# Eight key chunks per batch on VectorE and GpSimd, w2 in three loads, result columns in two PSUM tiles

## The chip, the core and the metric

The kernel runs on one core of a Trainium2 chip. The core has five engines that run side by side and meet at semaphores: TensorE (PE in the profile; its weight loads are listed as PEld), VectorE (DVE), ScalarE (ACT), GpSimd (POOL) and SyncE (SP), which here only issues transfers. Transfers between memory and SBUF are made by 16 DMA engines. A transfer of 128 rows is cut into 16 shares, one for each of them; this text calls the sixteen tracks on which these shares run one after the other *lanes*. TensorE writes to PSUM, and VectorE and ScalarE copy from there.

The metric is the device time of one execution in microseconds. Before the change three runs gave a median of 193.28 us (193.25 to 193.34).

## The reference

One decoding step for eight batch rows: a gated mix of an attention block and a small MLP, which read the same input.

```python
x = A_x                                     # [8, 1, 448]
g = sigmoid((x * gate_w).sum(-1))           # one gate per batch row
q = (x @ wq) as 16 heads of 256
k, v = the last 1024 positions of the caches, 8 heads, each used by 2 query heads
a = softmax(q k^T / 16) v, joined, @ wo
b = gelu(layernorm(x) @ w1 + b1) @ w2 + b2  # 448 -> 1792 -> 448
return g * a + (1 - g) * b                  # [8, 1, 448], bfloat16
```

The keys and values are 8 batches x 8 heads x 1024 positions x 256 numbers in bfloat16, 4 MB each per batch; wq, wo, w1 and w2 add 10.6 MB. In all 77.67 MB are read.

## The kernel before, in words

**Transfers.** All large loads go through SP's queue into a ring of four SBUF slots of 4 MB, in the order that the list `plan` gives: keys of batch 0, wq, then keys of batch b and values of batch b-1 by turns, then w1, the values of the last batch with w2 behind them, and wo. `pump` issues the next load when `done` has given a slot back. A key or value slot is filled by two loads of 2 MB (`kv_loader`, line 128), one for each group of four heads. w1, and later w2, share one slot (`w12`): w2 is issued by `last_values` (line 157) after the last values as one load of 128 rows of 12,544 B, into columns of that slot that nothing else uses. wo comes in seven pieces (line 140), the last four of them small, so that the last matmuls wait for little. Each load signals a semaphore; eight semaphores go round, and a load is issued only when the one eight places before it has landed.

**Keys.** `transpose_keys(b)` turns the keys of a batch so that the head dimension lies on the partitions. A batch has two halves of 32 chunks of 128 columns (`kn`, read as 4-byte words), and the work goes in 16 groups of four chunks (`CB = 4`). Groups 1 to 15 go through TensorE: four transposes into a PSUM tile `ktp` (line 360), then one copy to the SBUF tile `kt`, by ScalarE for the groups in `BY_ACT` (line 366) and by VectorE for the others (line 368). Group 0 goes another way, `turn_blocks`: VectorE turns 32x32 blocks into the tile `B` (line 330), and GpSimd puts the blocks in their places in `kt` with 16 copies (line 338). The steps of the softmax of the batch before are emitted between the groups, by the table `steps`: exp on ScalarE after group 0, its turning on VectorE after group 2, and so on.

**Attention.** `scores(b)` (line 427) multiplies the turned keys with the queries into `S_ps`; it needs all of `kt`. `top` takes the maximum on VectorE (`nmx`, line 440), `expo` the exponentials on ScalarE (`E`, line 444), `turn` turns them on VectorE (`EB`, line 451), `scale` and `bring` make the weights `ET`, and `values` (line 498) multiplies them with the values into `PO`. `finish` and `spread` (lines 511 to 524) put the result of a batch into `oP`.

**The tail.** After the last scores, `mlp_hidden` makes the hidden layer `hs`; `A1` is cleared (line 617); `values`, `finish` and `spread` end the last batch. Then the output matmuls run: 14 on w2 and 26 on wo, 448 columns wide, into `A1` on four row groups (line 632), whose sums VectorE takes to `accs` (line 639); then the last six chunks of wo, four matmuls of 112 columns each, and between them `accs` summed by `pick`, all into `A2` (line 643). `A2` holds the four column quarters on four groups of partitions. VectorE copies the first two quarters to `res0` and SP sends them; ScalarE copies the other two to `res1` and sends them from its own queue (lines 656 and 657).

Of the kernel before, what the change touches and what calls it, by code (L numbers as in the profile page):

```python
# [12 lines left out]
F32 = mybir.dt.float32  # L13
# [4 lines left out]
def kernel(  # L18
# [15 lines left out]
    nc = tc.nc  # L34
    P = nc.NUM_PARTITIONS

    NB, Sq, D = A_x.shape
# [8 lines left out]
    QD = 4  # L46
    BL = P // QD
# [7 lines left out]
    FB = FQ // BL  # L55
# [4 lines left out]
    SK = P // QD  # L60
    NCK = W // SK
    CB = 4
    UR = NG * rep
    HALF = D // 2
    DO = D // QD
# [16 lines left out]
    epool = ctx.enter_context(tc.tile_pool(name="epool", bufs=1))  # L82
# [3 lines left out]
    ps_kt = ctx.enter_context(tc.tile_pool(name="ps_kt", bufs=3, space=PSUM))  # L86
# [15 lines left out]
    def done(n=1):  # L102
        consumed[0] += n
        pump()
# [5 lines left out]
    def slot(*key):  # L110
        return slots[index[key]]

    def kv_loader(src, b, cuts=(1, 1), inner=False):
        pieces = [
            (i, k, cuts[i])
            for i in range(NG)
            for k in range(cuts[i])
        ]
        if inner:
            pieces.sort(key=lambda x: x[1])  # L120

        def load(t):
            for i, k, m in pieces:
                v = src[b, i * QD : (i + 1) * QD, kv_base:Sk, :].rearrange(
                    "a (s c) d -> s a (c d)", c=NCK
                )
                n = HS // m
                nc.sync.dma_start(  # L128
                    t[:, i * HS + k * n : i * HS + (k + 1) * n],
                    v[:, :, k * n : (k + 1) * n],  # L130
                )

        return load
# [15 lines left out]
    w2_v = B_w2.rearrange("(p c) n -> p (c n)", c=FB)  # L149
    wo_v = A_wo.rearrange("(q p j) n -> p q (j n)", p=P, j=J8)  # L150
    OW1T = NR * F
    OW2 = OW1T + FH
    wq_r = [wq_m[:, r * HD : (r + 1) * HD] for r in range(NR)]

    def last_values(t):
        kv_loader(A_v_cache, NB - 1, (2, 2), True)(t)
        nc.sync.dma_start(slot("w12")[:, OW2 : OW2 + FB * D], w2_v)

    add(("k", 0), kv_loader(A_k_cache, 0, (2, 1)))
    add(("wq",), rows_loader(wq_r + [wq_t]))  # L160
    for b in range(1, NB):
        add(("k", b), kv_loader(A_k_cache, b))
        add(("v", b - 1), kv_loader(A_v_cache, b - 1))
    add(("w12",), rows_loader([w1_m, w1_t]))
    add(("v", NB - 1), last_values)
    cuts = [(q, 0, J8) for q in range(NQW - 2)] + [
        (NQW - 2, 0, 4),
# [32 lines left out]
    nc.gpsimd.memset(xw[:], 0.0)  # L200
    qw = consts.tile([P, NJ, NB, QD, 2 * UR], BF16)
    nc.vector.memset(qw[:], 0.0)
# [120 lines left out]

    KT = {}

    BY_ACT = (1, 3, 4, 6, 7, 8, 10, 11, 13, 15)

    def turn_blocks(kn, kt, c0):
        B = epool.tile([P, CB, QD, SK // QD, QD], F32, tag="B", name="B")
        nc.vector.transpose(  # L330
            B[:].rearrange("p c w s a -> p (c w s a)"),
            kn[:, c0 * P : (c0 + CB) * P],
        )
        S8 = SK // QD
        words = kt[:].bitcast(F32)
        for w in range(QD):
            for g in range(QD):
                nc.gpsimd.tensor_copy(  # L338
                    words[BL * w : BL * (w + 1), :, c0 : c0 + CB, g * S8 : (g + 1) * S8, 0],
                    B[BL * g : BL * (g + 1), :, w].rearrange("p c s a -> p a c s"),  # L340
                )

    def transpose_keys(b, between=None):
        between = between or {}
        kn = slot("k", b)[:].bitcast(F32)
        for hh in range(NG):
            kt = ktpool.tile([P, QD, NCK, SK, NJ], BF16, tag="kt", name="kt")
            KT[hh] = kt
            for i in range(NCK // CB):
                g = hh * (NCK // CB) + i  # L350
                if g == 0:
                    turn_blocks(kn, kt, 0)
                    for step in between.get(g, ()):
                        step()
                    continue
                ktp = ps_kt.tile([P, CB, P, NJ], BF16, tag="ktp", name="ktp")
                words = ktp[:].bitcast(F32)
                for c in range(CB):
                    o = (hh * NCK + i * CB + c) * P
                    nc.tensor.transpose(  # L360
                        words[:, c, :, 0], kn[:, o : o + P], ident_f[:]
                    )
                dst = kt[:, :, i * CB : (i + 1) * CB, :, :]
                src = ktp[:].rearrange("p c (s a) t -> p a c s t", a=QD)
                if g in BY_ACT:
                    nc.scalar.copy(dst, src)  # L366
                else:
                    nc.vector.tensor_copy(dst, src)  # L368
                for step in between.get(g, ()):
                    step()  # L370
        done()
# [49 lines left out]
    def scores(b):  # L421
        CQ = QN // SK
        for n in range(W // QN):
            for u in range(NG):
                for j in range(NJ):
                    for t in range(QD):
                        nc.tensor.matmul(  # L427
                            S_ps[BL * t : BL * t + UR, n * QN : (n + 1) * QN],
                            lhsT=qw[:, j, b, t, rep * u : rep * u + UR],
                            rhs=KT[u][:, t, n * CQ : (n + 1) * CQ, :, j],  # L430
# [23 lines left out]
    def scale(b):  # L454
        EB = soft.pop(b)
        rs = spool.tile([P, BL], F32, tag="rs", name="rs")
        nc.vector.stream_shuffle(rs[:], EB[:, NCK, :], [0] * BL)
        sc = spool.tile([P, UR], F32, tag="sc", name="sc")
        nc.vector.reciprocal(sc[:], rs[:, 0:UR])
        nc.vector.tensor_scalar_mul(sc[:], sc[:], gall[:, b : b + 1])  # L460
        EZ = spool.tile([P, NCK, UR], BF16, tag="EZ", name="EZ")
        nc.vector.tensor_tensor(  # L462
# [117 lines left out]
    def steps(b):  # L580
# [15 lines left out]
        return d  # L596

    transpose_keys(0, {7: [moments]})
    gate()
    query()  # L600
    scores(0)
    top(0)
    for b in range(1, NB):
        transpose_keys(b, steps(b - 1))
        scores(b)
        top(b)
        values(b - 1)
# [11 lines left out]
    finish(b)  # L619
    spread(b)  # L620

    A2 = ps_kt.tile([P, DO], F32, tag="ktp", name="A2")
    w2 = slot("w12")
    w = slot("wo")
    NCH = NQW * J8
# [4 lines left out]
    for i, (lhsT, rhs) in enumerate(wide):  # L630
        g = i % QD
# [9 lines left out]
    for i, (lhsT, rhs) in enumerate(narrow):  # L641
        for t in range(QD):
            nc.tensor.matmul(
                A2[BL * t : BL * t + NB, :],
                lhsT=lhsT,
                rhs=rhs[:, t * DO : (t + 1) * DO],
                start=(i == 0),
                stop=(i == TAIL),
            )
    for h, (eng, copy) in enumerate(  # L650
        ((nc.sync, nc.vector.tensor_copy), (nc.scalar, nc.scalar.copy))
    ):
        res = consts.tile([NB, 2, DO], BF16, name=f"res{h}")
        for i in range(2):
            t = 2 * h + i
            copy(res[:, i, :], A2[BL * t : BL * t + NB, :])  # L656
        eng.dma_start(
            out_f[:, h * HALF : (h + 1) * HALF], res[:].rearrange("b i d -> b (i d)")
        )
# [30 lines left out]
```

## Time and profile before

| | before |
|---|---|
| median of three runs | 193.28 us |
| profiled execution's own time | 193.19 us |
| its span in the profile | 191.4 us |
| DMA: mean rate over the span | 407 GB/s |
| TensorE busy | 119.1 us (62%) |
| VectorE busy | 108.7 us (57%) |
| ScalarE busy | 91.9 us (48%) |
| GpSimd busy | 55.4 us (29%) |
| ScalarE's copies of turned keys, 80 of them | 76.1 us, mean 1024 ns |
| GpSimd's copies of turned keys, 128 of them | 51.3 us, mean 401 ns |
| VectorE's turn of group 0, 8 of them | 5.7 us, mean 711 ns |
| last piece of wo landed | 187.03 us |
| first and second half of the result landed | 189.47 and 190.06 us |

The times in the lower rows and in all profile lines are microseconds from the start of the span; the mean of one instruction is in nanoseconds. The page shows the span in 40 slices of 4.8 us: one digit for a slice is the busy share in tenths. q1 is SP's DMA queue, q10 ScalarE's; q8 and q14 are the queues that fetch instructions. A line of the timeline gives start, length, engine, line of the kernel, operation, output and inputs, count, and in brackets how long the engine had been idle before and what ended that. A line of the chain gives start, length and what the end of the kernel waited for then.

### The profile page before, as it was taken

The numbers are of one execution on the slowest core, as the hardware profiler recorded it, in microseconds if no ns is written. First come the engines' busy times: TensorE is split into PE (matmuls) and PEld (weight loads), VectorE is DVE, ScalarE is ACT, GpSimd is POOL, SyncE is SP. The second block draws the span as 40 slices with busy tenths as digits, with TensorE's granted clock in tenths as the row PEclk, the third lists the DMA queues.
The fourth block names the chain that finished last, engine by engine and source line by source line (L and its number), as shares of the span: only waits on it lengthen the run. The fifth ranks groups of instructions, "written<-read, shape, count | busy, mean of one in ns | idle before, by whom it ended". The sixth has DMA issues, their size and how long they took to land.

```text
span 191.4 us, 2916 instructions
## 1 busy us (share of the span) xinstructions
PE 119.1 (62%) x1114; PEld 77.0 (40%) x1114; DVE 108.7 (57%) x248; ACT 91.9 (48%) x105; POOL 55.4 (29%) x143
## 2 busy tenths in 40 slices
PE   0658509679784397738773676669854885083552
PEld 0646104555671185317641563168514761010111
DVE  4284673964889467705870687037822885847311
ACT  2298420894992259525852594228822892000001
POOL 8480000570750066005700480049002910000000
PEclk9999855999999969996999999756997999855555
DMA  5999999999999999999999999999999999999980
GB/s 204 445 402 425 440 435 419 425 421 432 422 430 428 428 421 431 426 431 428 418 431 425 421 435 428 428 428 416 431 431 428 425 425 420 403 422 430 407 321 3
DMA packets 7129, 77.86 MB, mean 407 GB/s; under 512 B 830, under 2 KB 1228, under 8 KB 1996
## 3 DMA queue, kind: packets, MB, share of 16 engines
q1 hardware_dynamic: 7072, 77.67, 96.3%
q8 instruction: 8, 0.13, 0.3%
q14 instruction: 5, 0.04, 0.1%
q10 hardware_dynamic: 44, 0.02, 0.0%
HBM read 77.67 MB, written 0.01 MB: 406 GB/s over the span
## 4 chain that ended last, share of the span: by engine, by line
DMA 73%; PE 10%; DVE 7%; ACT 4%; SPq 2%; issue 2%; DVEq 0%; ACTq 0%
DMA slot<-in_A_k_cache_dram 42%; DMA slot<-in_A_v_cache_dram 14%; DMA slot<-in_A_wq_dram 9%; DMA slot<-in_A_wo_dram 8%; PE ktp L360 7%; ACT kt L366 3%; DVE kt L368 2%; PE S_ps L427 2%; DVE qw L419 1%; SPq L128 1%; SPq L140 1%; DVE EZ L462 1%; PE S_ps L391 1%; DVE qt L404 1%; DVE nmx L440 1%
## 5 line engine op out<-in xcount | busy, mean ns | idle before, releaser
L366 ACT COPY kt<-ktp 128x1024 bf16<-128x1024 bf16 x80 | 76.1, 1024 | 37.0 <-PE ktp L360 36.9
L360 PE MATMUL ktp<-ident_f,slot 128*128 128x128 f32 x480 | 71.7, 305 | 31.4 <-DMA slot<-in_A_k_cache_dram 22.9
L360 PEld LDWEIGHTS ktp<-ident_f,slot 128*128 128x128 f32 x480 | 60.2, 157 | 49.2 <-issue 23.6
L338 POOL COPY kt<-B 32x128 f32<-32x128 f32 x128 | 51.3, 401 | 97.8 <-DVE B L330 86.3
L368 DVE COPY kt<-ktp 128x1024 bf16<-128x1024 bf16 x40 | 27.5, 689 | 16.9 <-PE ktp L360 16.5
L498 PE MATMUL PO<-slot,ET 128*16 128x512 bf16 x256 | 18.1, 429 | 16.2 <-DMA slot<-in_A_v_cache_dram 16.2
L444 ACT ACTIVATE E<-S_ps,nmx 128x1024 f32<-128x1024 f32 x8 | 8.9, 1114 | 28.7 <-DVE nmx L440 28.7
L330 DVE STREAM_TRANSPOSE B<-slot 128x512 f32<-128x512 f32 x8 | 5.7, 711 | 29.7 <-DMA slot<-in_A_k_cache_dram 29.6
L427 PE MATMUL S_ps<-kt,qw 128*4 128x512 bf16 x256 | 17.9, 419 | 5.4 <-DVE qw L419 5.4
L498 PEld LDWEIGHTS <-ET 128*16 128x16 bf16 x256 | 6.1, 94 | 27.6 <-DMA slot<-in_A_v_cache_dram 21.0
L440 DVE TENSOR_REDUCE nmx<-S_ps 128x1 f32<-128x1024 f32 x8 | 9.8, 1222 | 10.0 <-PE S_ps L427 10.0
L427 PEld LDWEIGHTS <-qw 128*4 128x4 bf16 x256 | 6.6, 85 | 14.0 <-DVE qw L419 6.5
L451 DVE STREAM_TRANSPOSE EB<-E 128x1056 f32<-128x1056 f32 x8 | 10.2, 1271 | 1.3 <-ACT E L444 1.3
L524 DVE TENSOR_TENSOR oP<-Y 32x32 bf16<-32x32 f32 x32 | 9.4, 295 | 1.1
L656 ACT CAST res<-A 8x112 bf16<-8x112 f32 x2 | 0.5, 246 | 15.8 <-DVE res L656 15.8
L481 DVE TENSOR_TENSOR ET<-sm,mask 128x512 bf16<-128x512 f32 x8 | 5.5, 692 | 2.2 <-PE sm L473 2.1
L511 DVE STREAM_TRANSPOSE T<-PO 128x512 f32<-128x512 f32 x8 | 5.7, 709 | 1.0 <-PE PO L498 0.9
L566 ACT ACTIVATE zb<-za 128x448 f32<-128x448 f32 x1 | 0.6, 577 | 10.8 <-DVE za L565 10.8
L473 PE MATMUL sm<-EZ,perm 128*128 128x128 bf16 x8 | 1.7, 216 | 6.0 <-DVE EZ L462 5.9
L632 PE MATMUL A<-slot,oP 128*8 128x448 bf16 x26 | 3.5, 547 | 2.5 <-DMA slot<-in_A_wo_dram 2.5
L639 DVE TENSOR_TENSOR accs<-A,b2s 128x448 f32<-128x448 f32 x1 | 0.6, 624 | 7.1 <-PE A L632 7.1
L516 DVE TENSOR_TENSOR Y<-T 64x64 f32<-64x64 f32 x16 | 4.0, 248 | 0.5
(91 smaller groups left out, 58.1 us busy)
## 6 DMA issues: line engine op xcount, KB each, us to landing
slot<-in_A_k_cache_dram SPq DMA_DIRECT2D x15, 2048.0 KB, 28.1
slot<-in_A_v_cache_dram SPq DMA_DIRECT2D x14, 2048.0 KB, 30.2
slot<-in_A_v_cache_dram SPq DMA_DIRECT2D x4, 1024.0 KB, 23.9
slot<-in_A_wq_dram SPq DMA_DIRECT2D x3, 1024.0 KB, 17.1
slot<-in_A_k_cache_dram SPq DMA_DIRECT2D x2, 1024.0 KB, 6.4
slot<-in_A_wo_dram SPq DMA_DIRECT2D x2, 896.0 KB, 18.7
slot<-in_B_w_dram SPq DMA_DIRECT2D x1, 1568.0 KB
slot<-in_B_w_dram SPq DMA_DIRECT2D x1, 1344.0 KB, 26.4
```

What stands on the lines that cost most here:

```text
L330: nc.vector.transpose(B[:].rearrange("p c w s a -> p (c w s a)"), kn[:, c0 * P : (c0 + CB) * P],)
L338: nc.gpsimd.tensor_copy(words[BL * w : BL * (w + 1), :, c0 : c0 + CB, g * S8 : (g + 1) * S8, 0], B[BL * g : BL * (g + 1), :, w].rearrange( ...
L360: nc.tensor.transpose(words[:, c, :, 0], kn[:, o : o + P], ident_f[:])
L366: nc.scalar.copy(dst, src)
L368: nc.vector.tensor_copy(dst, src)
L427: nc.tensor.matmul(S_ps[BL * t : BL * t + UR, n * QN : (n + 1) * QN], lhsT=qw[:, j, b, t, rep * u : rep * u + UR], rhs=KT[u][:, t, n * CQ ...
L440: nc.vector.reduce_max(nmx[:], S_ps[:], axis=AXIS.X, negate=True)
L444: nc.scalar.activation(E[:, 0:W], S_ps[:], ACT.Exp, bias=soft.pop(b)[:], scale=1.0, accum_out=E[:, W : W + 1],)
L451: nc.vector.transpose(EB[:].rearrange("p c r -> p (c r)"), E[:])
L498: nc.tensor.matmul(PO[BL * t : BL * t + Hq], lhsT=ET[:, c].rearrange("p u a r -> p (u a r)"), rhs=vn[:, c], start=(c < QD), stop=(c >= NCK ...
L511: nc.vector.transpose(T[:], PO[:].rearrange("p u (e j) -> p u j e", j=J8))
L524: nc.vector.tensor_tensor(oP[BL * i : BL * (i + 1), :, :, b], Yv[0:BL, :, :, i], Yv[BL : 2 * BL, :, :, i], op=ALU.add,)
```

## The change

Three edits.

1. VectorE and GpSimd take the first eight chunks of a batch's keys, two groups instead of one. `turn_blocks` works on `CP = 8` chunks: one turn of 1024 words per partition instead of 512, and 16 copies of 256 words instead of 128. Group 1 leaves `BY_ACT`, so TensorE transposes 14 groups and ScalarE copies nine; VectorE still copies five. The table `steps` has nothing for group 1.
2. w2 is loaded in three transfers: partitions 0 to 111, 112 to 119 and 120 to 127. Bytes and places are the same.
3. `A2` becomes two PSUM tiles. Quarters 0 and 1 go to the first, quarters 2 and 3 to the second, on the same partitions as before; VectorE copies from the first, ScalarE from the second.

```diff
+    CP = 8
...
     def last_values(t):
         kv_loader(A_v_cache, NB - 1, (2, 2), True)(t)
-        nc.sync.dma_start(slot("w12")[:, OW2 : OW2 + FB * D], w2_v)
+        for p0, p1 in ((0, P - 16), (P - 16, P - 8), (P - 8, P)):
+            nc.sync.dma_start(slot("w12")[p0:p1, OW2 : OW2 + FB * D], w2_v[p0:p1, :])
...
-    BY_ACT = (1, 3, 4, 6, 7, 8, 10, 11, 13, 15)
+    BY_ACT = (3, 4, 6, 7, 8, 10, 11, 13, 15)
 
     def turn_blocks(kn, kt, c0):
-        B = epool.tile([P, CB, QD, SK // QD, QD], F32, tag="B", name="B")
+        B = epool.tile([P, CP, QD, SK // QD, QD], F32, tag="B", name="B")
         nc.vector.transpose(
             B[:].rearrange("p c w s a -> p (c w s a)"),
-            kn[:, c0 * P : (c0 + CB) * P],
+            kn[:, c0 * P : (c0 + CP) * P],
         )
...
-                    words[BL * w : BL * (w + 1), :, c0 : c0 + CB, g * S8 : (g + 1) * S8, 0],
+                    words[BL * w : BL * (w + 1), :, c0 : c0 + CP, g * S8 : (g + 1) * S8, 0],
...
-                if g == 0:
-                    turn_blocks(kn, kt, 0)
+                if g < CP // CB:
+                    if g == 0:
+                        turn_blocks(kn, kt, 0)
...
-    A2 = ps_kt.tile([P, DO], F32, tag="ktp", name="A2")
+    A2 = [ps_kt.tile([P, DO], F32, tag="ktp", name="A2") for h in range(2)]
...
-                A2[BL * t : BL * t + NB, :],
+                A2[t // 2][BL * t : BL * t + NB, :],
...
-            copy(res[:, i, :], A2[BL * t : BL * t + NB, :])
+            copy(res[:, i, :], A2[h][BL * t : BL * t + NB, :])
```

## The prediction

> **What bounds the kernel now.** I read the page's slices and queues first, for whether the transfers ever pause.
>
> ```profile
> DMA  5999999999999999999999999999999999999980
> GB/s 204 445 402 425 440 435 419 425 421 432 422 430 428 428 421 431 426 431 428 418 431 425 421 435 428 428 428 416 431 431 428 425 425 420 403 422 430 407 321 3
> ...
> q1 hardware_dynamic: 7072, 77.67, 96.3%
> q8 instruction: 8, 0.13, 0.3%
> ...
> q10 hardware_dynamic: 44, 0.02, 0.0%
> ```
>
> They don't, from 5 us on, until the last slices. The kernel ends when its 77.67 MB have arrived, plus a tail. The chain of waits gives that tail:
>
> ```profile
> 145.91 25.96 DMA slot<-in_A_v_cache_dram
> ...
> 171.89 14.57 DMA slot<-in_A_wo_dram
> ...
> 186.51 1.15 PE A L643 x31
> 187.65 0.25 DVE res L656
> ...
> 188.29 0.07 ACT res L656
> ```
>
> So work on the keys can move the end only by letting the transfers starve or by coming late at 186.5. Third, the timeline: one steady batch, and the last microseconds.
>
> ```profile
> 126.15 0.71 DVE L330 STREAM_TRANSPOSE B<-slot 128x512 f32<-128x512 f32 x1 [6.53 <-DMA slot<-in_A_k_cache_dram]
> ...
> 127.02 7.04 POOL L338 COPY kt<-B 32x128 f32<-32x128 f32 x16 [12.49 <-DVE B L330]
> ...
> 137.34 1.97 PE L427 MATMUL S_ps<-kt,qw 128*4 128x512 bf16 x32
> ...
> 140.68 1.11 ACT L444 ACTIVATE E<-S_ps,nmx 128x1024 f32<-128x1024 f32 x1 [2.22 <-DVE nmx L440]
> ...
> 145.99 0.71 DVE L330 STREAM_TRANSPOSE B<-slot 128x512 f32<-128x512 f32 x1 [5.40 <-DMA slot<-in_A_k_cache_dram]
> ...
> 187.64 0.56 DVE L656 CAST res<-A 8x112 bf16<-8x112 f32 x2 [1.03 <-PE A L643]
> 188.23 0.36 SPq L657 DMA_DIRECT2D out_dram<-res  x1
> 188.29 0.50 ACT L656 CAST res<-A 8x112 bf16<-8x112 f32 x2 [15.77 <-DVE res L656]
> 188.82 0.31 ACTq L657 DMA_DIRECT2D out_dram<-res  x1
> ```
>
> GpSimd ends at 134.06, 3.3 us ahead of the scores; ScalarE's copies start only after VectorE's, though they read other columns.
>
> Last, the landings. The trace has the moment at which each of a transfer's 16 shares (lanes) lands. w2: seven at 176.16 to 177.01, eight at 177.71 to 177.95, one at 178.14. This spacing is the same from transfer to transfer, so a lane keeps its place, until an instruction fetch holds it. The eight q8 fetches (1.03 to 1.11 us) each put another lane back by about 1.55 us: the group of eight. The last lane was put back twice, by 0.97 us at 29.0 and 132.2, with 8 KB fetches of q14. That this lane is a low one shows in b1's load: four rows, four packets, and the one at 48.358 lies within 4 ns of this lane's packet border; the three other lanes so found, and b2's single one among the four, are in the early group. So lanes 0 to 3 are three early ones and the very last one.
>
> **Key groups.** Per batch ScalarE loses one copy (1.02 us) and TensorE four transposes; both are idle by 141.9 each batch, so nothing is gained at the end. VectorE turns 1024 columns instead of 512: L330 takes 0.711 us for 512, L451 1.271 us for 1056, so 1.24 us, 0.53 us more. GpSimd's 16 copies double to 256 elements. A one-element MEMSET takes 98 ns, so from 0.098 + 2 x 0.303 = 0.704 us to 2 x 0.401 = 0.802 us each, plus 0.04 us between; 11.9 to 13.5 us a batch instead of 7.04. I take the upper, since the longer a copy the less the fixed part weighs. Scores wait for all 16: in the batch shown 126.15 + 1.24 + 0.16 + 13.5 = 141.05 instead of 137.34, 3.7 us late. Behind them in the queues are nmx (VectorE), exp (ScalarE) and the values (TensorE): 4.55 us from scores to exp's end, so 145.6, before the next keys at 145.99. GpSimd's loop with scores, nmx and VectorE's turn is 13.5 + 2.0 + 1.3 + 1.4 = 18.2 us, under the batch's 19.6 us of transfer. The values free a slot up to 3.7 us later (up to 5 us in batches 1 and 2, where GpSimd starts at 35.65); but a load lands 28 to 30 us after its issue, against 9.8 us of its own transfer, so some 18 us of cover. Cost: nothing. In the last batch scores move from 156.63 to 160.9 and VectorE's chain with them: the memset of A1 ends at 179.7 instead of 175.42, oP is ready at 182.25 instead of 178.88. TensorE, done with w2 at 181.4, then has wo's pieces that landed at 180.32, 182.53 and 183.65 to catch up, 8 + 8 + 4 matmuls (0.92, 0.92, 0.55 us): done at 184.65, before the piece of 184.79. Cost again nothing, with 0.2 us to spare.
>
> **w2 in three.** A packet of 16,384 B takes 613 ns, so a row of 12,544 B 0.47 us. Now each lane has eight rows. The 112 rows make seven on each. The page's q10 row says what eight rows do: 44 packets are a data and a completion packet for each of 8 + 1 + 1 + 4 + 8 rows (x, gate_w, b2, b1, half the output), so eight rows use eight lanes, which I take as the lowest, since b1's four hold b2's one. Lanes 0 to 7 then have nine rows, the others seven. The transfers behind (wo) keep each lane's place. The lower bound: each single row costs 0.47 us, and the last lane, a low one, lands 0.47 us later. The upper: the only eight-row load on neighbouring rows here is x: 7,168 B, in 105 ns from first start to last end; 14 times the bytes is 1.47 us, twice 2.94, less the 0.47 of the row taken away: +2.47 us. For the lower speaks that x's packets took 39 to 42 ns, as b1's and b2's alone (41); for the upper, that the group is stretched. Below nothing, -0.47, only if the last lane were a high one; b1 speaks against it. Neither row is nearer; I take the middle, two loads of 0.97 us: +1.47 us. The end follows one for one: wo's sixth piece landed at 186.46 on the same lane and TensorE went on at 186.51.
>
> [...]
>
> SP issues two DMAs more (0.33 us each). Each issue of wo waited for a landing eight transfers back; now it is six of the old order, so the sixth waits for w2's first part (about 178) and the seventh for the second (at most 181); their data are due at 182.9 and 184.0. Nothing. The matmuls on w2 wait for three landings; they are 1.66 us, and the next piece comes 2.2 us later: nothing.
>
> **Two result tiles.** ScalarE can start with VectorE, at 187.68 instead of 188.29; its DMA goes out at 188.21 instead of 188.82. Then SP's (issued 188.23, landed 189.47) is last instead of ScalarE's (landed 190.06): -0.59 us. Bounds: 0, if ScalarE still waits, and -0.59, since SP's path is untouched. I take -0.59, as the diff leaves nothing shared.
>
> **Sum.** +1.47 - 0.59 = +0.88 us. The profiled execution took 193.19 us (span 191.4), 0.09 under the median of 193.28: 194.07 by the one, 194.16 by the other; I say 194.1.
>
> **Rivals.**
> - The single rows cost only 0.47 us each: +0.47 - 0.59 = -0.12, 193.2, no change that can be told (0.2% is 0.39 us). For it: x's 39 to 42 ns a packet.
> - The other side: the last lane is not among the eight, so the nine late lanes lose a row while the early ones, 1.1 us ahead, take it up: -0.47 - 0.59 = -1.06, 192.2. For it: seven of the eight early or low lanes are indeed ahead. Against it: the packet border at 48.358. The early lanes (177.01 at the latest) pass 178.14 themselves from 0.8 us a single row on; there it ends.
> - GpSimd becomes the bound of the tail: at more than 0.81 us a copy the 0.2 us are used up, and at 1.0 us scores and oP come 3.2 us later still; the wide matmuls end at 188.6 instead of 185.94: +2.7 - 0.59, 195.4. Against it: 401 ns for twice 128 elements.
> - ScalarE still waits: the forecast without -0.59, 194.7.
>
> **Numbers.** Forecast with its own range 193.7 to 195.2 (0.75 us a single row to the upper bound): 0.50, ScalarE's wait inside it. Rows at 0.47 us: 0.26. Last lane high: 0.18. GpSimd: 0.06. So faster 0.18, same 0.26, slower 0.56. The range takes the gaining case in and goes to the upper bound, 193.28 + 2.47 - 0.59: 192.2 to 195.2.
>
> **What would show it.** Landings of w2's two small parts: 0.47 or 0.97 or 1.47 us apart on a lane; the last landing of wo near 188.5 (187.03 before); L338 at 0.70 to 0.80 us; scores 2 to 4 us later with the DMA row still at 9; both CASTs starting together. Wrong would make it: instruction fetches falling on other lanes, a granted clock other than 0.50 in the last 10 us, or the late lane escaping the crowd of the early ones.

## The result: 2.8% slower, and the profile after

The changed kernel takes 198.74 us, the median of five runs (198.64 to 199.11), against 193.34 us (193.25 to 193.81) for the kernel before beside it: 1.028 times, with a 95% interval of 1.0264 to 1.0296. The profiled execution took 198.64 us, its span 196.8 us; before it was 193.19 and 191.4. So 5.45 us are lost, where the prediction had 0.88 lost and at most 1.9. Slower was right; the size was not, and the time lies outside the range.

The page's slices of the kernel after, one value for each 4.9 us, and the queue that carries the loads:

```profile
DMA  5999999999999999999999999999999999999980
GB/s 210 428 421 425 433 426 424 423 426 436 424 424 426 433 426 431 429 423 426 426 429 429 423 426 426 429 418 433 429 429 423 426 414 414 426 237 196 354 330 6
...
q1 hardware_dynamic: 7088, 77.67, 96.4%
```

The bytes are the same, and the row of busy digits is the same to the last figure. The row below it is not: in the slices from 172 to 182 us the rate falls to 237 and 196 GB/s, from 414 to 436 in the slices before (the first, 210, is the start). The lanes hardly pause (share 1.12, 1.04 and 0.90 in the windows below), but each packet takes longer (a row of w2 885 ns in the median, 472 before). A reader who looks at the busy row alone sees nothing.

The windows of the same stretches show it more finely (start and end, length, busy time and count of TensorE's matmuls, its weight loads, VectorE, ScalarE and GpSimd, granted clock, DMA share, GB/s). Of before:

```profile
172.00:175.00 3.00, 0.59 (x8) 0.25 (x12) 2.25 (x5) 0.53 (x1) 0.00 (x0) 0.50 1.01 425
175.00:180.00 5.00, 2.95 (x30) 0.56 (x19) 2.75 (x8) 0.00 (x0) 0.00 (x0) 0.50 1.00 415
180.00:184.00 4.00, 2.14 (x20) 0.56 (x20) 0.00 (x0) 0.00 (x0) 0.00 (x0) 0.50 1.01 402
```

Of after:

```profile
172.00:175.00 3.00, 2.01 (x17) 0.40 (x16) 2.27 (x4) 0.36 (x1) 0.00 (x0) 0.50 1.12 271
175.00:180.00 5.00, 1.89 (x16) 0.40 (x16) 4.39 (x11) 0.21 (x1) 0.00 (x0) 0.50 1.04 216
180.00:184.00 4.00, 0.00 (x0) 0.00 (x0) 0.50 (x2) 0.00 (x0) 0.00 (x0) 0.50 0.90 212
```

The granted clock stays at 0.50 and the DMA share within about a tenth of 1.0, while the rate falls to some two thirds and then, from 175 us on, to half. Between 180 and 184 TensorE has nothing to do: w2 is not there. These are the microseconds in which w2 travels. The end of the chain of waits says the same:

```profile
123.16 32.53 DMA slot<-in_A_v_cache_dram
...
155.71 26.93 DMA slot<-in_B_w_dram
...
182.66 9.74 DMA slot<-in_A_wo_dram
...
192.45 1.16 PE A L646 x32
```

A load of w2 (the DRAM tensor `B_w` in the chain) has taken a place between the values and wo. The sixth piece of wo is waited for until 192.40 us, where it was 186.46 before.

The packet records and the moments at which a load's sixteen shares land give the sizes (us; a row's packets in ns):

| | before | after |
|---|---|---|
| last landing of the last values | 174.37 | 175.92 |
| w2, all of it | 176.16 to 178.14 | |
| w2, 112 rows | | 178.34 to 182.64 |
| w2, second and third part, last landing | | 183.60, 184.35 |
| last landing of wo | 187.03 | 192.97 |
| last half of the result landed | 190.05 | 195.58 |
| a row of w2, 12,544 B, on its lane | 469 to 480 ns, median 472 | 469 to 1,386 ns, median 885 |

So the transfers end 5.94 us later, and the tail behind them is 2.61 us instead of 3.02: 5.94 - 0.41 = 5.53 us, the whole difference to within 0.1 us (5.45 by the two executions' times, 5.4 by their spans).

One question is left by the trace: what makes a row slow? It can be where the rows lie, the number of loads, that a load uses eight lanes only, or what else the change does in the same microseconds.

### The profile page after: what moved, and what is told of

It reads as the page before. It is cut to its first block, busy times and chain, and to the rows that moved or that the text cites. A ratio compares the mean times of both kernels' runs of the same rounds, so it can differ in the third digit from the quotient of the medians.

```text
span 196.8 us, 2845 instructions
## 1 busy us (share of the span) xinstructions
PE 120.9 (61%) x1082; PEld 77.3 (39%) x1082; DVE 124.5 (63%) x248; ACT 84.7 (43%) x97; POOL 83.7 (43%) x143
## 4 chain that ended last, share of the span: by engine, by line
DMA 57%; POOL 15%; PE 13%; DVE 5%; ACT 4%; issue 3%; SPq 1%; POOLq 0%; ACTq 0%
DMA slot<-in_A_v_cache_dram 35%; POOL kt L340 15%; DMA slot<-in_B_w_dram 14%; PE S_ps L430 6%; DMA slot<-in_A_wo_dram 5%; PE ktp L363 4%; DMA slot<-in_A_k_cache_dram 4%; PE PO L501 3%; ACT kt L369 2%; DVE qw L422 1%; DVE nmx L443 1%; ACT E L447 1%; ACT L269 1%; ACT L250 1%; DVE B L332 1%
## 5 line engine op out<-in xcount | busy, mean ns | idle before, releaser
L340 POOL COPY kt<-B 32x256 f32<-32x256 f32 x128 | 79.6, 622 | 73.5 <-DVE B L332 37.6
L369 ACT COPY kt<-ktp 128x1024 bf16<-128x1024 bf16 x72 | 69.0, 1020 | 37.7 <-PE ktp L363 37.7
L363 PEld LDWEIGHTS ktp<-ident_f,slot 128*128 128x128 f32 x448 | 59.4, 164 | 51.3 <-issue 29.0
L430 PE MATMUL S_ps<-kt,qw 128*4 128x512 bf16 x256 | 20.9, 476 | 16.0 <-POOL kt L340 10.2
L332 DVE STREAM_TRANSPOSE B<-slot 128x1024 f32<-128x1024 f32 x8 | 9.9, 1241 | 19.2 <-DMA slot<-in_A_k_cache_dram 19.1
L501 PE MATMUL PO<-slot,ET 128*16 128x512 bf16 x256 | 17.1, 410 | 4.1 <-DMA slot<-in_A_v_cache_dram 4.1
L430 PEld LDWEIGHTS <-qw 128*4 128x4 bf16 x256 | 7.4, 93 | 26.3 <-issue 14.5
L527 DVE TENSOR_TENSOR oP<-Y 32x32 bf16<-32x32 f32 x32 | 15.8, 494 | 1.1
L519 DVE TENSOR_TENSOR Y<-T 64x64 f32<-64x64 f32 x16 | 8.4, 527 | 0.6
L635 PE MATMUL A<-slot,hs 128*8 128x448 bf16 x14 | 1.7, 568 | 6.6 <-DMA slot<-in_B_w_dram 6.6
```

The source lines that it names most:

```text
L332: nc.vector.transpose(B[:].rearrange("p c w s a -> p (c w s a)"), kn[:, c0 * P : (c0 + CP) * P],)
L340: nc.gpsimd.tensor_copy(words[BL * w : BL * (w + 1), :, c0 : c0 + CP, g * S8 : (g + 1) * S8, 0], B[BL * g : BL * (g + 1), :, w].rearrange( ...
L363: nc.tensor.transpose(words[:, c, :, 0], kn[:, o : o + P], ident_f[:])
L430: nc.tensor.matmul(S_ps[BL * t : BL * t + UR, n * QN : (n + 1) * QN], lhsT=qw[:, j, b, t, rep * u : rep * u + UR], rhs=KT[u][:, t, n * CQ ...
L501: nc.tensor.matmul(PO[BL * t : BL * t + Hq], lhsT=ET[:, c].rearrange("p u a r -> p (u a r)"), rhs=vn[:, c], start=(c < QD), stop=(c >= NCK ...
L519: nc.vector.tensor_tensor(Y[:, :, u, :], T[0 : 2 * BL, u, :, k], T[2 * BL : P, u, :, k], op=ALU.add)
```

## The experiments

The expectations below were written when the result was known, and before the kernel in question ran. In short, the first theory in them, later called A, is that w2's loads alone make the loss; that lanes which write neighbouring partitions hold each other up is my guess at the cause, and no run shows the place. By it a cut by columns, which leaves every load all 128 rows, should cost nothing. Against it stand the other parts of the change, the number of loads or of issues, and the load on eight lanes as such. A ratio is taken against the runs of the kernel before that lie beside it on the same chip; where these spread (193.16 to 194.75 in the second group, 193.19 to 194.91 in the first), it can be somewhat under the quotient of the medians.

### The parts one by one

**w2 in three parts alone**, on the kernel before:

```diff
-        nc.sync.dma_start(slot("w12")[:, OW2 : OW2 + FB * D], w2_v)
+        for p0, p1 in ((0, P - 16), (P - 16, P - 8), (P - 8, P)):
+            nc.sync.dma_start(slot("w12")[p0:p1, OW2 : OW2 + FB * D], w2_v[p0:p1, :])
```

> The kernel before with w2 loaded as 112, 8 and 8 rows and nothing else changed. Theory 1 (the loads of w2 carry the whole loss; in the changed kernel the first part's rows took 0.8 to 0.95 us each instead of 0.47 and the last piece of wo landed at 192.97 instead of 187.03): last landing of wo about 5.9 us later, time about 199.2 us. Rival (the key groups carry most of it: scores late, VectorE's small sums slower, and w2's slow packets follow from that): under 195 us.

Measured: 199.65 us (199.30 to 200.49) beside 193.57, a ratio of 1.0308 [1.0275, 1.0341]. The last wo landed at 192.94 us, 5.91 later than before. The 112 rows landed from 178.38 to 182.49, the single rows until 184.27; the rows took 900 ns in the median. In its window of 175 to 180 us:

```profile
175.00:180.00 5.00, 1.88 (x16) 0.40 (x16) 2.43 (x7) 0.00 (x0) 0.00 (x0) 0.50 1.07 224
```

The rate is 224 GB/s, as in the changed kernel. The whole loss is here, without the other two edits. It is even somewhat more, since the gain of the two result tiles is missing.

**Two result tiles alone:**

```diff
-    A2 = ps_kt.tile([P, DO], F32, tag="ktp", name="A2")
+    A2 = [ps_kt.tile([P, DO], F32, tag="ktp", name="A2") for h in range(2)]
...
-                A2[BL * t : BL * t + NB, :],
+                A2[t // 2][BL * t : BL * t + NB, :],
...
-            copy(res[:, i, :], A2[BL * t : BL * t + NB, :])
+            copy(res[:, i, :], A2[h][BL * t : BL * t + NB, :])
```

> The kernel before with only the two result tiles. By the step of the prediction: both CASTs start together, ScalarE's half leaves 0.6 us earlier, 0.59 us less, 192.7 us. Rival (the two small stores now go out together and land later than SP's alone did, as in the changed kernel, where they landed 2.61 us after the last wo instead of 3.03): 0.4 us less, 192.9 us.

Measured: 193.04 us (192.85 to 194.00) beside 193.57; 0.9965 [0.9944, 0.9985]. The last microseconds of its timeline:

```profile
187.72 0.54 DVE L656 CAST res<-A 8x112 bf16<-8x112 f32 x2 [1.03 <-PE A L643]
187.76 0.50 ACT L656 CAST res<-A 8x112 bf16<-8x112 f32 x2 [15.17 <-PE A L643]
188.29 0.37 SPq L657 DMA_DIRECT2D out_dram<-res  x1
188.30 0.32 ACTq L657 DMA_DIRECT2D out_dram<-res  x1
```

ScalarE now waits for TensorE, not for VectorE's `res`, and both stores go out together. But from the last wo to the last store landed it is 187.11 to 189.73, 2.62 us, where it was 3.02 before: a gain of 0.40, not 0.59. The reason is at the far end. Before, the stores left 0.59 us apart and each landed 1.23 us after its issue. In the changed kernel, where they leave 0.01 us apart, SP's lands after 1.25 and ScalarE's after 1.42 us: the later of the two takes 0.19 us more from its issue than before.

**Eight chunks of keys alone:**

```diff
+    CP = 8
...
-    BY_ACT = (1, 3, 4, 6, 7, 8, 10, 11, 13, 15)
+    BY_ACT = (3, 4, 6, 7, 8, 10, 11, 13, 15)
...
-            kn[:, c0 * P : (c0 + CB) * P],
+            kn[:, c0 * P : (c0 + CP) * P],
...
-                if g == 0:
-                    turn_blocks(kn, kt, 0)
+                if g < CP // CB:
+                    if g == 0:
+                        turn_blocks(kn, kt, 0)
```

> The kernel before with only the eight chunks on VectorE and GpSimd. Theory 1: scores 1 to 2 us later in every batch, oP of the last batch about 1 us later and caught up before the fourth piece of wo; the transfers never pause; 193.3 us, within 0.2%. Rival: the late scores or the slower sums reach the end, 194 to 198 us.

Measured: 193.27 us (193.14 to 193.35) beside 193.57; 0.9977 [0.9964, 0.9991]. Its fastest run and the fastest of before are 0.05 us apart and the last wo lands at 187.08 instead of 187.03, so I read this as no effect on the end, not as a gain. The slices:

```profile
DMA  5999999999999999999999999999999999999980
GB/s 195 450 411 419 443 430 425 411 428 439 421 426 431 414 435 431 426 425 431 414 438 428 428 428 421 425 431 419 435 428 418 431 428 416 411 424 423 407 319 2
```

The rate holds to the end, although GpSimd's copies have grown to 624 ns each and the scores wait for them.

**The change without its w2 edit**, the two edits above together:

> The changed kernel with w2 loaded whole again. Theory 1: all of the loss is gone and the gain of the two result tiles is left, 192.7 to 192.9 us, faster than the kernel before. Rival: 194 us or more, what the key groups cost less the result tiles' gain.

Measured: 192.91 us (192.77 to 192.99) beside 193.57; 0.9954 [0.9937, 0.9971]. The last wo landed at 187.15, the last store at 189.76. This version beats both kernels: what the change has to give is the two result tiles, and what it costs is w2 in three.

### What makes the rows slow

**Three loads of all 128 rows**, cut by columns: 12, 1 and 1 of the 14 chunks that a row of w2 holds here, so 10,752, 896 and 896 B of every row:

```diff
-        nc.sync.dma_start(slot("w12")[:, OW2 : OW2 + FB * D], w2_v)
+        for c0, c1 in ((0, 12 * D), (12 * D, 13 * D), (13 * D, FB * D)):
+            nc.sync.dma_start(slot("w12")[:, OW2 + c0 : OW2 + c1], w2_v[:, c0:c1])
```

> The kernel before with w2 in three loads of all 128 rows, cut by columns (rows of 10,752, 896 and 896 B). [...] Rival B (three loads in place of one, or small loads, cost by themselves): 1 us or more of the 5.9.

Measured: 193.57 us (193.49 to 193.71) beside 193.34; 0.9995 [0.997, 1.002]. Last wo at 187.24. Rows of 10,752 B took 404 to 415 ns, those of 896 B 41 ns; in its window:

```profile
175.00:180.00 5.00, 3.00 (x30) 0.64 (x19) 2.76 (x8) 0.00 (x0) 0.00 (x0) 0.50 1.01 405
```

So two more loads, two more issues and SP's later waits cost nothing that the times can tell, and 0.2 us at most by the last wo (187.03 before). In these runs the rows of a load matter, not how many loads there are: three loads of w2 cut by rows took 199.65 us, three cut by columns 193.57.

**Two halves**, 64 rows each:

```diff
-        nc.sync.dma_start(slot("w12")[:, OW2 : OW2 + FB * D], w2_v)
+        for p0, p1 in ((0, P // 2), (P // 2, P)):
+            nc.sync.dma_start(slot("w12")[p0:p1, OW2 : OW2 + FB * D], w2_v[p0:p1, :])
```

> The kernel before with w2 as two loads of 64 rows. [...] Rival B': only shares that are no power of two (112 rows, seven each) or loads on eight lanes are slow: no change, 193.3 us. [...]

Measured: 198.18 us (198.05 and 198.32) beside 193.34; 1.0207 [1.0108, 1.0306]. Rows took 469 to 1,282 ns, 920 in the median; the two halves' last landings were 180.09 and 183.72, the last values' 176.91, the last wo's 192.37: 5.3 us late. From 175 to 180 us the DMA share was 0.97 at 206 GB/s, so hardly a lane paused, and a load of half the partitions is as slow as one of 112 (920 ns a row against 885). Part of the delay stands in the values: their last share landed 2.54 us late, though nothing about them was changed. While a slow load ran, the packets of other loads on other lanes were slow too: in the changed kernel the rows of the last values (8,192 B) took up to 636 ns from 171.9 us on, where before they took 321 at most, and those of wo (7,168 B) up to 891 before 184 us, where they took 287 at most before the change.

Next come loads that nothing reads, into columns of that slot that nobody uses, issued behind the whole w2; the kernel's result is as before. What they vary is which rows one load takes: the partitions that it writes, and with them its rows of w2 in DRAM, since one index picks both. The first two have the same 32 rows of 7,680 B on partitions 0 to 31, in four loads of eight:

```diff
         nc.sync.dma_start(slot("w12")[:, OW2 : OW2 + FB * D], w2_v)
+        X0 = OW2 + FB * D
+        n = SLOT - X0
+        for j in range(4):
+            rows = slice(8 * j, 8 * j + 8)
+            nc.sync.dma_start(slot("w12")[rows, X0:SLOT], w2_v[rows, 0:n])
```

> The kernel before with four more loads behind w2, each of eight neighbouring rows (partitions 0 to 7, 8 to 15, 16 to 23, 24 to 31; 7,680 B of w2 to spare columns of the slot, read by nothing). A row takes 0.29 us alone, so four rows put lanes 0 to 7 back by 1.15 us if the lanes do not disturb each other. [...] Rival (eight-row loads are as fast as others, the loss is the 112 rows alone): 1.2 us later, 194.5 us.

and, with every load on every fourth partition:

```diff
-            rows = slice(8 * j, 8 * j + 8)
+            rows = slice(j, BL, 4)
```

> As spare_next, the same 32 rows and bytes, but each of the four loads takes every fourth partition of the first 32. [...] Rival C (a load on eight lanes is slow by itself, wherever its rows lie): the same as spare_next.

Measured: neighbours 196.28 us (196.23 and 196.33) beside 193.34, 1.0109 [1.0012, 1.0206]; every fourth 194.87 us (194.67 to 195.47), 1.0062 [1.0033, 1.0091]. The windows, neighbours first:

```profile
175.00:180.00 5.00, 1.21 (x16) 0.17 (x12) 3.70 (x10) 0.00 (x0) 0.00 (x0) 0.50 1.03 300
```

```profile
175.00:180.00 5.00, 3.02 (x30) 0.78 (x23) 4.08 (x11) 0.00 (x0) 0.00 (x0) 0.50 1.00 415
```

300 against 415 GB/s, for the same bytes to the same 32 partitions in the same number of loads on eight lanes each. Neighbouring rows took 291 to 682 ns, 445 in the median, and w2's own rows beside them up to 1,048; rows on every fourth partition took 291 to 298 ns and w2's at most 481. The last wo landed at 189.94 and at 188.41. So a load on eight lanes is not slow as such: at 291 to 298 ns its rows took no longer than those of 128 rows in the table below.

The second of them also tells which lanes those eight are. Its eight landings end at 176.50, 176.66, 177.19, 177.21, 177.23, 178.10, 178.10 and 178.65 us: five of w2's early lanes, two of its late group, and the very last one, which went on from w2's 178.36. The eight hold the last lane, as predicted, but five early ones, not seven.

**The form of the 112 rows by itself**, with all 128 rows beside it, and 64 rows as every second partition. Each is one load of 7,680 B a row behind the whole w2:

```diff
         nc.sync.dma_start(slot("w12")[:, OW2 : OW2 + FB * D], w2_v)
+        X0 = OW2 + FB * D
+        n = SLOT - X0
+        rows = slice(0, P)
+        nc.sync.dma_start(slot("w12")[rows, X0:SLOT], w2_v[rows, 0:n])
```

> The kernel before with one more load behind w2: all 128 rows of 7,680 B, to the spare columns of the slot, read by nothing. Eight rows a lane at the 0.29 us that a row of this length took in spare_step: 2.3 us later, 195.6 us, by both theories. It is the measure for the next two.

```diff
-        rows = slice(0, P)
+        rows = slice(0, P - 16)
```

> The same with the first 112 rows only. By the prediction's step (seven rows a lane at the usual price): 2.0 us, 195.3 us, less than spare_128. Theory A (the seven rows of a lane no longer lie so that the lanes keep out of each other's way): rows take 0.55 us in the middle, about as much longer as w2's 0.885 against 0.47; 3.8 us or more, 197 us, so fewer bytes take longer than spare_128.

```diff
-        rows = slice(0, P)
+        rows = slice(0, P, 2)
```

> The same with every second partition, 64 rows over all of SBUF, four a lane: 1.2 us at the usual price, 194.5 us. [...]

| load behind w2 | time, us | beside it | ratio [95%] | its rows, ns | it landed | last wo |
|---|---|---|---|---|---|---|
| 128 rows | 195.33 | 193.28 | 1.0104 [1.0074, 1.0133] | 291 to 304 | 180.52 | 189.42 |
| 112 rows | 197.65 | 193.28 | 1.0224 [1.0194, 1.0254] | 291 to 626, median 530 | 183.21 | 191.89 |
| 64 rows, every second | 194.16 | 193.28 | 1.0052 [1.0035, 1.0069] | 291 to 305 | 179.26 | 188.16 |

The windows of the 128 rows, of the 112 and of the 64:

```profile
175.00:180.00 5.00, 2.16 (x26) 0.41 (x15) 3.09 (x10) 0.00 (x0) 0.00 (x0) 0.56 0.98 411
180.00:184.00 4.00, 0.92 (x8) 0.23 (x8) 0.00 (x0) 0.00 (x0) 0.00 (x0) 0.50 1.01 418
```

```profile
175.00:180.00 5.00, 1.69 (x24) 0.30 (x16) 2.76 (x8) 0.00 (x0) 0.00 (x0) 0.50 1.03 278
180.00:184.00 4.00, 1.31 (x14) 0.26 (x7) 0.00 (x0) 0.00 (x0) 0.00 (x0) 0.50 0.98 296
```

```profile
175.00:180.00 5.00, 2.91 (x26) 0.57 (x19) 2.69 (x8) 0.00 (x0) 0.00 (x0) 0.50 1.00 416
```

An eighth fewer rows make the load 2.7 us longer, and the kernel 2.3 us slower: one load in both, nothing else changed. And 64 rows that are spread over all partitions run at 416 GB/s, where w2 in 64 rows that lie together had 206 in the same window. In the slow run w2's own rows, which are still on their way, take up to 948 ns.

**112 and 16 rows**, to split the loss between the large part and the eight-row form:

```diff
-        nc.sync.dma_start(slot("w12")[:, OW2 : OW2 + FB * D], w2_v)
+        for p0, p1 in ((0, P - 16), (P - 16, P)):
+            nc.sync.dma_start(slot("w12")[p0:p1, OW2 : OW2 + FB * D], w2_v[p0:p1, :])
```

> The kernel before with w2 as 112 and 16 rows. Theory A: the 112 rows land at about 182.5 as in the three-part kernel, and the 16 rows, one on each lane and four lanes on neighbouring partitions, cost more than a row too: 5 to 6 us later, 198.5 to 199.5 us. Rival (the eight-row loads make a large part of the loss): 112 rows as slow, but the end 1.5 us or more earlier than with the two eight-row loads, under 198 us.

Measured: 198.03 us (197.94 and 198.11) beside 193.28; 1.0243 [1.0214, 1.0273]. All 128 rows together took 889 ns in the median. The shares of the 112 rows landed at 182.50 at the latest; those of the 16 landed 0.92 to 1.66 us behind them (in order of landing), at 183.59 at the latest. The last wo came at 192.22, 0.72 us earlier than with twice eight rows. So the form of eight rows costs some 0.7 us more than sixteen in one load, and most of the loss has been made by the time that the 112 are in.

### What is shown, and what is not

Shown: the loss is w2's loads alone, and in them it is which rows one load takes together. 128 rows, every second row, or every fourth of 32 run at the usual price for each packet (291 to 305 ns a row of 7,680 B); eight, 64 or 112 that lie side by side take 1.5 to 2 times as long in the median (445 and 530 ns for eight and 112 such rows; 920 for 64 rows of w2, which took 472 before), and the other loads beside them are slow too (in the changed kernel the rows of the last values took up to 636 ns, 321 at most before).

Not shown: that it is the place in SBUF. In every run here the partitions of a load and its rows in DRAM moved together, so the reading side is a rival that no run excludes. Nor was a load of 112 rows run that do not lie side by side: whether their number, seven to a lane, or their lying together makes them slow is open, and which lane takes which of the 112 rows was not read from any run.

## Why the prediction was wrong, point by point

**The step that failed** is "The 112 rows make seven on each", at the price given two sentences earlier: "A packet of 16,384 B takes 613 ns, so a row of 12,544 B 0.47 us". The count fits (112 rows over 16 landings) and the price was wrong: 885 ns in the median of w2's rows. I had counted this part as one usual row fewer on each lane, and put all the doubt on the 16 rows left over. For loads of 128 rows the price is exact (472 ns before), and I took it over to a load of another shape without a bound. The last landings let the loss be followed, taking the lane that ends last as the same one in both: the values end 1.55 us late (175.92 against 174.37), because lanes that were ahead were in w2 already (its first row starts at 171.87 us, and from 171.9 on rows of the values took up to 636 ns). Then seven rows take 182.64 - 175.92 = 6.72 us, 0.96 each, where the eight of before took 178.14 - 174.37 = 3.77, 0.47 each. That is 1.55 + 6.72 - 3.77 = 4.50 us when the 112 rows are in, where the prediction had one usual row less, -0.47. The two small parts add 184.35 - 182.64 = 1.71, where it had 1.94. Of the 6.21 us at w2's end (184.35 against 178.14), 5.94 arrive at the end of wo.

**The single rows** were taken at 0.97 us between 0.47 and 1.47; the shares of the two small parts landed 0.75 to 1.30 us apart (in order of landing), six of eight over 0.97, inside the bounds. On the last landings, 1.71 us against 1.94, this term of the sum held; it had been taken as the middle of two bounds, so that it came so near is in part luck. The rival at 0.47 is out.

**The cut by rows.** An eight-row load cost 1.30 us at most, between the landings of the two small parts, and still the time was longer than predicted, since the large part had been left at the usual price. Every w2 cut by rows that was tried cost 4.7 us or more, the cut by columns some 0.2.

**Which lanes.** The last lane is among the eight that an eight-row load uses: right, so the gaining rival falls. "Seven of the eight early" was wrong: it is five. It mattered little, since all lanes were slow: the 112 rows, seven on a lane, landed from 178.34 to 182.64 us, eight rows on a lane before from 176.16 to 178.14. The prediction also named instruction fetches on other lanes as a way to be wrong, and one of q8 did fall into w2's time, at 174.96 us (in the kernel before, the last one ahead of the output was at 164.42). With w2's edit alone it was at 164.50 and the loss the same, so it is not the cause.

**SP's issues.** The sixth of wo was to wait until about 178 and the seventh until 181 at most; the waits are longer (three of SP's issues, 7.3 us in all, the longest 6.4):

```profile
SPq L141 <- DMA slot<-in_B_w_dram: 7.3, 3, 6.4
```

They follow from w2's late landings: 182.66 and 183.62. The sixth then landed 9.74 us after its issue, behind what was already in the queue, so I count nothing for them; no run tells them apart from the late landings.

**Key groups cost nothing:** right, and shown by the run with this edit alone. Its terms were less good. A copy of 256 elements takes 622 ns, below my lower bound of 704. Doubling 401 ns added 221, so the fixed part is some 180 ns (an estimate, if the rest grows with the elements), not the 98 ns of a MEMSET. The groups of the page (line, engine, operation, shapes, count, then busy time, mean ns, and idle time ahead with what ended it) and the batch of the prediction in the timeline, of after:

```profile
L340 POOL COPY kt<-B 32x256 f32<-32x256 f32 x128 | 79.6, 622 | 73.5 <-DVE B L332 37.6
```

```profile
127.56 10.56 POOL L340 COPY kt<-B 32x256 f32<-32x256 f32 x16 [8.94 <-DVE B L332]
138.17 1.99 PE L430 MATMUL S_ps<-kt,qw 128*4 128x512 bf16 x32 [1.29 <-POOL kt L340]
141.53 1.11 ACT L447 ACTIVATE E<-S_ps,nmx 128x1024 f32<-128x1024 f32 x1 [3.60 <-DVE nmx L443]
145.99 1.25 DVE L332 STREAM_TRANSPOSE B<-slot 128x1024 f32<-128x1024 f32 x1 [4.55 <-DMA slot<-in_A_k_cache_dram]
```

The scores do wait for GpSimd, but start at 138.17 instead of 141.05 as worked out, 0.8 us later than before. In the last batch they start at 157.97 (156.63 before), well ahead of the 160.9 of the prediction. The spare of 0.2 us was worked out too low as well: in the run with the key groups alone oP is ready at 179.08 us (178.88 before), not at 182.25. The rival in which GpSimd sets the tail needed 0.81 us a copy; it is out. The chain of after passes through GpSimd's copies for 15% of the span, and still the run with this edit alone, whose copies are as long, ends when the kernel before does: a step on the chain that other waiting covers is no loss.

**Two result tiles:** the copies start together, as predicted, and SP's path is untouched up to its issue. The rival in which ScalarE still waits is out. The term was -0.59 and measured -0.40 to -0.41, because the two stores now travel together. The timeline of after:

```profile
193.58 0.54 DVE L659 CAST res<-A 8x112 bf16<-8x112 f32 x2 [1.04 <-PE A L646]
193.62 0.50 ACT L659 CAST res<-A 8x112 bf16<-8x112 f32 x2 [18.41 <-PE A L646]
194.15 0.32 SPq L660 DMA_DIRECT2D out_dram<-res  x1
194.16 0.32 ACTq L660 DMA_DIRECT2D out_dram<-res  x1
```

**The sum, put right:** +5.94 for w2, 0 for the keys, -0.41 for the tiles: +5.53, against 5.45 measured.

## What to carry to other kernels

A packet's price belongs to the shape of the load it was read from: a row of w2 took 472 ns in the median in one load of 128 rows, and 885 in the three of the changed kernel. Before a load is cut, ask which rows each piece takes: keep pieces at all 128 rows and cut columns (193.57 us here beside 193.34), or step the rows so that they spread over the partitions (291 to 305 ns a row here, 530 in the median for 112 side by side); a block of neighbouring rows is to be measured first. And read the transfer's rate beside the busy share, since lanes whose packets are slow look fully busy (share 1.04 at 216 GB/s here, 1.00 at 415 before).

## What the runs showed that was not expected

Fewer rows can take longer: 112 rows of 7,680 B landed 2.7 us after the time of 128 of them (183.21 against 180.52 us). A load that is slow by its rows also slows what runs beside it: the last values landed 1.55 us late in the changed kernel and 2.54 us late with w2 in halves.

Two groups of VectorE's sums took longer than before, 494 and 527 ns in the mean instead of 295 and 248. The page's groups of after:

```profile
L527 DVE TENSOR_TENSOR oP<-Y 32x32 bf16<-32x32 f32 x32 | 15.8, 494 | 1.1
...
L519 DVE TENSOR_TENSOR Y<-T 64x64 f32<-64x64 f32 x16 | 8.4, 527 | 0.6
```

The same four sums, in the batch where GpSimd is at its copies (twelve from 150.04 to 157.92 us) and in the one where it has none left:

```profile
155.36 2.72 DVE L527 TENSOR_TENSOR oP<-Y 32x32 bf16<-32x32 f32 x4
...
167.46 1.27 DVE L527 TENSOR_TENSOR oP<-Y 32x32 bf16<-32x32 f32 x4
```

It cost nothing at the end here (508 and 509 ns in the run with the keys alone, which ends as before), but a kernel that VectorE bounds could lose by it; no run here shows that.
